# The first narrowing operation of the attention stage: on ScalarE and issued ahead, or on VectorE and in its turn

## The chip, the core and the metric

One core of a Trainium2 chip runs the whole program. The metric is device time in microseconds (us), lower is better. The core's engines are PE (matrix products; PEld is its weight load), DVE (VectorE), ACT (ScalarE), POOL (GpSimd) and SP (SyncE, which here issues the loads and stores). Each engine runs its own instructions strictly in the order in which the program lists them; an instruction whose input is late holds up everything behind it on that engine.

## The reference

```python
q_d = q.reshape(B, H, Sd, 4, D).mean(axis=3)            # k_d, v_d alike
out_up = np.repeat(sm_attn(q_d, k_d, v_d), 4, axis=2)   # attention on means of 4
mask = np.abs(pos[:, None] - pos[None, :]) < 4
out_local = softmax(where(mask, scale * q @ k.T, -1e9)) @ v
x = (out_up + out_local) as [2304, 512]                 # B=4, H=8, S=576, D=64
logits = x @ phi;  slots = softmax(logits, 0).T @ x     # 32 slots, 8 experts
slot_out[e] = relu(slots[e] @ w1[e]) @ w2[e]
y = softmax(logits, 1) @ slot_out
h = relu(y @ w_in);  result = (h * h) @ w_out           # w_in, w_out in float64
```

The last two weights come as 64-bit floats (512 x 2048 and 2048 x 512), and the kernel makes 32-bit floats of them.

## The kernel before

The work comes in four stages: attention (to about 200 us), the gate and the expert layers (to about 250 us), the first part of the last feed-forward layer, and its main loop, which is half of the span and almost all PE.

**Attention** is 16 units u, each one pair of heads of one batch. A unit passes through a software pipeline of about four steps; step s (lines 701 to 723) works on units s to s-4 at once. `ORDER` lists what one step issues, a letter each: V, D, A are the value products, their scaling on ACT (`xd`, line 530) and the sum on DVE (`xt`, line 538); T transposes q and k on PE (`tr`) and copies them out on ACT (`qk`, line 384); P pairs the heads of the next unit (`qp` on ACT, `kp` on DVE, line 373); Q and L and 4 are loads of q and k, of v in windows (`vw`), and of v in groups of 4 (`v`, used on POOL in line 484, whose sum `vd` DVE finishes in line 490). The last three letters are l (loads of weights that later stages need, `LOADN` of them), and c, which calls `narrow_next` (line 277) as often as `CONV[s]` says. All loads go through SP's queue in program order. SP waits at a load until its buffer is free; the load of q, for one, waits until ACT has made `qp` of the unit whose buffer it takes.

**Narrowing** a weight piece (128 x 512 doubles) takes five operations (`narrow`, line 206): the absolute value of the high words (line 213, ACT), a clamp (line 214), a shift with a mask (line 215), the sign (line 216) and the low bits (line 217), the last four on DVE. Pieces are narrowed two at a time, a *turn*: `NORDER` gives the turns, of which the first four, eight pieces of w_in, lie in attention. `narrow_turn` issues one operation of both pieces at each call. `narrow_ahead` takes the next turn, if its loads have been issued, and issues its first operation at once; it is called when a turn begins, and again right after the second operation of the current turn (line 268). So a turn's first operation is issued two to four calls ahead of its second.

```python
yield nc.scalar.activation(out=dst, in_=hi.bitcast(F32), func=AF.Abs)
...
if count[0] == 2:
    narrow_ahead()
```

`xq` is None until a pool of that name is opened in the expert stage (line 894); it stays None through all of attention, and is set for the later turns.

Of the kernel before, what the change touches and what calls it, by code (L numbers as in the profile page):

```python
# [9 lines left out]
F32 = mybir.dt.float32  # L10
# [3 lines left out]
AF = mybir.ActivationFunctionType  # L14
ALU = mybir.AluOpType
# [20 lines left out]
MAG_HI = 1.875 * 2.0 ** 16 - 2.0 ** -7  # L36
FILL = {0: 8, 1: 16, 2: 10, 3: 0, 16: 5, 17: 2, 18: 2}
FILLN = 0
CONV = {3: 1, 4: 1, 5: 1, 6: 1, 7: 1, 8: 1, 9: 1, 10: 0, 11: 2, 12: 1, 13: 2, 14: 1, 15: 2}
FILLT = {16: 4, 17: 6, 18: 8}  # L40
TCH = 384
LOOK = 2
# [29 lines left out]
def attention_moe_ffn_kernel(  # L72
# [12 lines left out]
    nc = tc.nc  # L85
# [120 lines left out]
    def narrow(dst, raw):  # L206

        hi, lo = raw[:, :, 1], raw[:, :, 0]  # L210
        di = dst.bitcast(I32)
        two, sel2 = nc.vector.tensor_scalar, nc.vector.scalar_tensor_tensor
        yield nc.scalar.activation(out=dst, in_=hi.bitcast(F32), func=AF.Abs)
        yield two(out=dst, in0=dst, scalar1=MAG_LO, scalar2=MAG_HI, op0=ALU.max, op1=ALU.min)
        yield two(out=di, in0=di, scalar1=3, scalar2=0x3FFFFFF8, op0=ALU.logical_shift_left, op1=ALU.bitwise_and)
        yield sel2(out=di, in0=hi, scalar=-0x40000000, in1=di, op0=ALU.bitwise_and, op1=ALU.bitwise_or)
        yield sel2(out=di, in0=lo, scalar=29, in1=di, op0=ALU.logical_shift_right, op1=ALU.bitwise_or)

    def narrow_win(i, j):
        if (j, i // 2) not in win:  # L220
            pool, tag = place = min((x for x in free if x[0] is (wa if j < 2 else ring)), key=lambda x: x[0] is wa and x[1])
            free.remove(place)
            win[j, i // 2] = pool.tile([128, 2, FF // 4], F32, tag=tag, name=f"win{j}_{i // 2}")
        yield from narrow(win[j, i // 2][:, i % 2], got["win", i, j])
        done("win", i, j)
# [3 lines left out]
    def narrow_wout(f):  # L229
        w32[f] = xq.tile([128, DM], F32, tag="w32", bufs=W32, name=f"w32_{f}")  # L230
        yield from narrow(w32[f], got["wout", f, 0])
# [7 lines left out]
    current, count, ahead = [], [0], []  # L239

    def ready(y):
        if y[0] == "o":
            return ("wout", int(y[1:]), 0) in got and xq is not None
        return ("win", int(y[1]), int(y[3])) in got

    def narrow_ahead():

        if ahead or not turns or not all(ready(y) for y in turns[0]):
            return
        if len(w32) + sum(y[0] == "o" for y in turns[0]) > W32:  # L250
            return
        for y in turns.popleft():
            ahead.append((y, narrow_wout(int(y[1:])) if y[0] == "o" else narrow_win(int(y[1]), int(y[3]))))
        for y, z in ahead:
            next(z)

    def narrow_turn():
        if not current:
            narrow_ahead()
            if not ahead:  # L260
                return False
            current.extend(ahead)
            ahead.clear()
            count[0] = 1
        count[0] += 1
        for y, z in current:
            next(z)
        if count[0] == 2:
            narrow_ahead()
        if count[0] == 5:  # L270
            for y, z in current:
                next(z, None)
            current.clear()
            count[0] = 0
        return True

    def narrow_next(n=1):
        for _ in range(n):
            narrow_turn()

    def narrow_to(x):

        wanted = lambda y: y == f"o{x}" if isinstance(x, int) else y[0] == "w" and int(y[3]) <= int(x[1:])
        while any(wanted(y) for y, z in current + ahead) or any(wanted(y) for t in turns for y in t):
            assert narrow_turn()
# [4 lines left out]
    with tc.tile_pool(name="att", bufs=1, side="right") as ap:  # L290
# [410 lines left out]
        for s in range(3, NU):  # L701
# [6 lines left out]
            for x in ORDER:  # L708
# [9 lines left out]
                if x == "c":  # L718
                    narrow_next(CONV.get(s, 0))
                if x == "P" and s == NU - 2:  # L720
# [147 lines left out]
    for e in range(NE):  # L868
# [23 lines left out]
        if e == LBE:  # L892
            lb_scope.close()
            xq = ctx.enter_context(tc.tile_pool(name="slots", bufs=1, side="right", reuse_waits="tile"))
# [196 lines left out]
```

## Time and profile before

| | us |
|---|---|
| median of 3 runs (lowest, highest) | 486.12 (484.34, 487.14) |
| the profiled execution's own time | 488.41 |
| its span, first to last instruction | 486.6 |
| PE, DVE, ACT, POOL busy | 431.8, 312.9, 261.8, 96.7 |

Busy shares are means over stages that differ: after 280 us PE is hardly ever idle, before 200 us every engine waits at times. So the part to read is the stretch in which the changed instructions stand, about 35 to 200 us. The profiled execution's span is 1.8 us shorter than its time, and its time is 2.3 us above the median.

### The profile page before, as it was taken

The numbers are of one execution on the slowest core, as the hardware profiler recorded it, in microseconds if no ns is written. First come the engines' busy times: TensorE is split into PE (matmuls) and PEld (weight loads), VectorE is DVE, ScalarE is ACT, GpSimd is POOL, SyncE is SP. The second block draws the span as 40 slices with busy tenths as digits, with TensorE's granted clock in tenths as the row PEclk, the third lists the DMA queues.
The fourth block names the chain that finished last, engine by engine and source line by source line (L and its number), as shares of the span: only waits on it lengthen the run. The fifth ranks groups of instructions, "written<-read, shape, count | busy, mean of one in ns | idle before, by whom it ended". The sixth has DMA issues, their size and how long they took to land.

```text
span 486.6 us, 10625 instructions
## 1 busy us (share of the span) xinstructions
PE 431.8 (89%) x4098; PEld 330.7 (68%) x4098; DVE 312.9 (64%) x675; ACT 261.8 (54%) x657; POOL 96.7 (20%) x128
## 2 busy tenths in 40 slices
PE   4799788496996794999987999999999999999996
PEld 3577565384675663644455787878888888888885
DVE  5669778495997983313259899875555545546452
ACT  3576564564765542212466988786545444444442
POOL 4336555363544643002000000000000000000000
PEclk9687889797897896789999999999999999999999
DMA  7898988688897879799999200000200100100001
GB/s 146 204 277 210 202 235 203 178 217 206 191 234 194 249 208 286 252 362 399 393 408 409 112 0 3 0 1 24 107 1 1 66 0 8 58 1 30 35 2 65
DMA packets 65780, 75.13 MB, mean 154 GB/s; under 512 B 23873, under 2 KB 47169, under 8 KB 65729
## 3 DMA queue, kind: packets, MB, share of 16 engines
q1 hardware_dynamic: 65584, 74.31, 51.7%
q8 instruction: 32, 0.52, 0.5%
q14 instruction: 20, 0.16, 0.1%
q10 hardware_dynamic: 144, 0.13, 0.1%
HBM read 69.71 MB, written 4.72 MB: 153 GB/s over the span
## 4 chain that ended last, share of the span: by engine, by line
PE 62%; DVE 15%; DMA 9%; issue 6%; POOL 3%; ACT 2%; SPq 2%; DVEq 0%; POOLq 0%; ACTq 0%
PE po L1020 37%; DMA q<-in_q_dram 4%; PE hp L828 4%; PE so L852 3%; PE up L960 3%; DMA v<-in_v_dram 3%; DVE vd L490 2%; POOL v L484 2%; DMA k<-in_k_dram 2%; DVE kz L401 2%; PE tr L383 2%; PE av L512 1%; PE av L525 1%; PE sd L435 1%; PE ptp L478 1%
## 5 line engine op out<-in xcount | busy, mean ns | idle before, releaser
L1020 PE MATMUL po<-wparts,ghi 128*128 128x512 f32 x576 | 150.6, 395 | 4.3 <-DVE wparts L918 4.2
L1020 PEld LDWEIGHTS po<-wparts,ghi 128*128 128x128 f32 x576 | 107.2, 189 | 26.8 <-DVE wparts L918 6.6
L965 ACT ACTIVATE r<-up 128x384 f32<-128x384 f32 x96 | 47.0, 489 | 72.0 <-PE up L960 67.1
L1020 PE MATMUL po<-wparts,glo 128*128 128x512 f32 x288 | 82.2, 393 | 0.5 <-DVE glo L973 0.5
L969 DVE TENSOR_TENSOR r<-r 128x384 f32<-128x384 f32 x64 | 35.7, 558 | 58.4 <-ACT ghi L968 58.4
L973 DVE TENSOR_TENSOR glo<-r,ghi 128x384 fp32r<-128x384 f32 x94 | 52.4, 558 | 16.5 <-ACT ghi L972 10.4
L1020 PEld LDWEIGHTS po<-wparts,glo 128*128 128x128 f32 x288 | 54.4, 189 | 12.5 <-DVE glo L973 1.2
L968 ACT ACTIVATE ghi<-r 128x384 fp32r<-128x384 f32 x66 | 34.7, 526 | 2.1
L960 PE MATMUL up<-cst,ast 128*128 128x384 f32 x96 | 33.0, 346 | 0.4 <-DVE ast L951 0.4
L484 POOL TENSOR_TENSOR v<-v 72x512 f32<-72x512 f32 x16 | 20.7, 1293 | 51.7 <-DMA v<-in_v_dram 39.6
L490 DVE TENSOR_TENSOR vd<-v 72x256 f32<-72x256 f32 x16 | 16.0, 999 | 20.8 <-POOL v L484 20.8
L463 POOL TENSOR_TENSOR pl<-el,sm 64x350 f32<-64x350 f32 x30 | 24.4, 813 | 18.8 <-DVE sm L455 12.1
L525 PE MATMUL av<-pdt,vd 72*64 72x144 f32 x128 | 13.9, 348 | 15.8 <-DVE vd L490 15.8
L383 PE MATMUL tr<-ident,qp 96*128 96x96 f32 x96 | 20.1, 299 | 7.2 <-ACT qp L373 6.9
L384 ACT COPY qk<-tr 128x384 f32<-128x384 f32 x48 | 22.1, 523 | 6.6 <-PE tr L383 5.5
L512 PE MATMUL av<-pt,vw 64*64 64x58 f32 x640 | 23.8, 230 | 0.2 <-DVE xt L538 0.2
L512 PEld LDWEIGHTS av<-pt,vw 64*64 64x64 f32 x640 | 21.6, 144 | 3.2 <-issue 1.5
L478 PE MATMUL ptp<-ident,pl 128*128 128x128 f32 x80 | 15.6, 338 | 7.7 <-ACT qk L384 6.3
L383 PE MATMUL tr<-ident,kp 96*128 96x96 f32 x96 | 19.5, 293 | 2.3 <-DVE kp L373 2.3
L960 PEld LDWEIGHTS up<-cst,ast 128*128 128x128 f32 x96 | 18.1, 189 | 4.6 <-DVE ast L951 0.7
L401 DVE COPY kz<-qk 64x586 f32<-64x586 f32 x32 | 20.4, 636 | 1.0 <-ACT qk L384 0.8
L525 PEld LDWEIGHTS av<-pdt,vd 72*64 72x64 f32 x128 | 8.8, 160 | 17.8 <-DVE vd L490 12.3
(186 smaller groups left out, 726.9 us busy)
## 6 DMA issues: line engine op xcount, KB each, us to landing
w<-in_moe_w_dram SPq DMA_DIRECT2D x64, 512.0 KB
win<-in_moe_w_in_dram SPq DMA_DIRECT2D x16, 512.0 KB
wout<-in_moe_w_out_dram SPq DMA_DIRECT2D x16, 512.0 KB
q<-in_q_dram SPq DMA_DIRECT2D x16, 288.0 KB
k<-in_k_dram SPq DMA_DIRECT2D x16, 288.0 KB
v<-in_v_dram SPq DMA_DIRECT2D x16, 288.0 KB
out_dram<-o SPq DMA_DIRECT2D x17, 256.0 KB
vw<-in_v_dram SPq DMA_DIRECT2D x32, 128.0 KB
```

The lines of the kernel that those rows point to most:

```text
L383: nc.tensor.transpose(t[:, j, r], st[nm][:, i, r].rearrange("p h d -> p (h d)"), ident[0:96, 0:96])
L401: (nc.scalar.copy if h < KZACT else nc.vector.tensor_copy)(out=kz[r, h], in_=k2[r])
L484: nc.gpsimd.tensor_tensor(out=v4[:, :, 0], in0=v4[:, :, 0], in1=v4[:, :, 1], op=ALU.add)
L490: nc.vector.tensor_tensor(out=vd.rearrange("p h a d -> p (h a) d"), in0=v4[:, :, 0, 0], in1=v4[:, :, 0, 1], op=ALU.add)
L512: nc.tensor.matmul(av[a][rr, 2 * HQ * i:2 * HQ * i + 2 * HQ].rearrange("p (f c) -> p f c", f=2), vw[rr, 2 * i + a], ptv[rr, i, :, a, 0:HQ] ...
L525: nc.tensor.matmul(dn[rr], st["vd"][:, h, a], st["pdt"][:, a, :, h], start=(a == 0), stop=(a == 1), skip_group_check=True,)
L960: nc.tensor.matmul(t, ast[:, 128 * f:128 * f + 128], cst[:, c * n:c * n + n], start=True, stop=True)
L965: nc.scalar.activation(out=r, in_=t, func=AF.Relu)
L968: nc.scalar.activation(out=ghi, in_=r, func=AF.Square)
L969: nc.vector.tensor_tensor(out=g, in0=r, in1=r, op=ALU.mult)
L973: nc.vector.tensor_tensor(out=glo, in0=g, in1=ghi, op=ALU.subtract)
L1020: nc.tensor.matmul(po[c][i], a[:, 128 * i:128 * i + 128], w[f], start=(f == 0 and w is whi and a is ghi), stop=(f == NF - 1 and a is glo), ...
```

## The change

Where `xq` is None, that is in attention, the first operation of `narrow` is a bitwise AND on DVE (clearing the sign bit of the high word) in place of the ACT absolute value; `narrow_turn` ends its call after issuing it when it begins a new turn; and `narrow_ahead` is not called after the second operation. A turn so takes five calls where it took four. Four turns now need 20 calls where they needed 16: `CONV` has three more, one each in steps 8, 12 and 15, and of the three calls after step 15 two had found nothing to do before and one does now. So the same eight pieces are still done within attention. Later turns are as before.

```diff
-CONV = {3: 1, 4: 1, 5: 1, 6: 1, 7: 1, 8: 1, 9: 1, 10: 0, 11: 2, 12: 1, 13: 2, 14: 1, 15: 2}
+CONV = {3: 1, 4: 1, 5: 1, 6: 1, 7: 1, 8: 2, 9: 1, 10: 0, 11: 2, 12: 2, 13: 2, 14: 1, 15: 3}
...
-        yield nc.scalar.activation(out=dst, in_=hi.bitcast(F32), func=AF.Abs)
+        if xq is None:
+            yield two(out=di, in0=hi, scalar1=0x7FFFFFFF, scalar2=None, op0=ALU.bitwise_and)
+        else:
+            yield nc.scalar.activation(out=dst, in_=hi.bitcast(F32), func=AF.Abs)
...
     def narrow_turn():
         if not current:
+            new = not ahead
             narrow_ahead()
...
             count[0] = 1
+            if new and xq is None:
+                return True
         count[0] += 1
         for y, z in current:
             next(z)
-        if count[0] == 2:
+        if count[0] == 2 and xq is not None:
             narrow_ahead()
```

The order of instructions moves on ACT and DVE only; PE, POOL and SP keep theirs. Lines behind 213 stand 3 to 6 lines further down in the changed kernel.

ACT at the end of step 7, before: the last copies of that step, the first operation of the third turn (both pieces), then step 8's `xd`, the copies out of the transposes, and `qp`.

```order
L566 COPY xk_1270<-xp_1280 128x4x128
L569 COPY xr_1271<-xrp_1286 64x128
L213 ACTIVATE win_0_1300<-win_1_935 128x512
L213 ACTIVATE win_0_1300<-win_1_1294 128x512
L530 ACTIVATE xd<-av_0_1303 128x288
L384 COPY qk_136<-tr_0_1330 128x2x2x96
L384 COPY qk_136<-tr_1_1336 128x2x2x96
L384 COPY qk_136<-tr_2_1342 128x2x2x96
L373 COPY qp_1351<-q_1172 96x6x64 x2
```

The same place now:

```order
L572 COPY xk_1265<-xp_1275 128x4x128
L575 COPY xr_1266<-xrp_1281 64x128
L536 ACTIVATE xd<-av_0_1295 128x288
L390 COPY qk_136<-tr_0_1322 128x2x2x96
L390 COPY qk_136<-tr_1_1328 128x2x2x96
L390 COPY qk_136<-tr_2_1334 128x2x2x96
L379 COPY qp_1343<-q_1167 96x6x64 x2
```

Both ACTIVATE of line 213 are gone from between step 7 and step 8; nothing stands in their place on ACT.

DVE at the end of step 8, before: the normalisation, the second operation's follower of the second turn (line 215, both pieces), then step 9's `xt` and `kp`.

```order
L454 TENSOR_SCALAR sm_1390<-sm_1390 128x3
L455 RECIPROCAL sm_1390<-sm_1390 128x3
L215 TENSOR_SCALAR win_1_602<-win_1_602 128x512 x2
L538 TENSOR_TENSOR xt_1516<-av_0_1471,xd 128x5x58
L538 TENSOR_TENSOR xt_1516<-av_1_1472,xd 128x5x58
L373 COPY kp_1522<-k_1359 96x6x64 x2
```

The same place now:

```order
L460 TENSOR_SCALAR sm_1382<-sm_1382 128x3
L461 RECIPROCAL sm_1382<-sm_1382 128x3
L214 TENSOR_SCALAR win_1_1461<-win_0_329 128x512
L214 TENSOR_SCALAR win_1_1461<-win_0_327 128x512
L217 TENSOR_SCALAR win_1_1461<-win_1_1461 128x512 x2
L544 TENSOR_TENSOR xt_1511<-av_0_1466,xd 128x5x58
L544 TENSOR_TENSOR xt_1511<-av_1_1467,xd 128x5x58
L379 COPY kp_1517<-k_1351 96x6x64 x2
```

The new first operation (line 214 of the changed kernel) and the clamp (its line 217) of the second turn stand here now, two pairs where one stood. Step 12 has the same shape for the third turn.

DVE at the end of attention, before: the last operation of the fourth turn, then the `xt` of unit 14 and the `vd` of unit 15.

```order
L217 SCALAR_TENSOR_TENSOR win_1_2002<-win_1_1465,win_1_2002 128x512
L217 SCALAR_TENSOR_TENSOR win_1_2002<-win_1_1633,win_1_2002 128x512
L538 TENSOR_TENSOR xt_2864<-av_0_2820,xd 128x5x58
L538 TENSOR_TENSOR xt_2864<-av_1_2821,xd 128x5x58
L490 TENSOR_TENSOR vd_2877<-v_2812 72x256
```

The same place now:

```order
L219 SCALAR_TENSOR_TENSOR win_1_2683<-win_1_1457,win_1_2683 128x512
L219 SCALAR_TENSOR_TENSOR win_1_2683<-win_1_1628,win_1_2683 128x512
L544 TENSOR_TENSOR xt_2862<-av_0_2818,xd 128x5x58
L544 TENSOR_TENSOR xt_2862<-av_1_2819,xd 128x5x58
L220 SCALAR_TENSOR_TENSOR win_1_2683<-win_1_1457,win_1_2683 128x512
L220 SCALAR_TENSOR_TENSOR win_1_2683<-win_1_1628,win_1_2683 128x512
L496 TENSOR_TENSOR vd_2877<-v_2810 72x256
```

The fourth turn ends one call later: its last pair stands between the last `xt` shown and `vd`, where nothing stood.

## Rows read from the trace of the kernel before

**Rows 1.** The page, busy time by engine, and the chain by engine.

```profile
PE 431.8 (89%) x4098; PEld 330.7 (68%) x4098; DVE 312.9 (64%) x675; ACT 261.8 (54%) x657; POOL 96.7 (20%) x128
...
PE 62%; DVE 15%; DMA 9%; issue 6%; POOL 3%; ACT 2%; SPq 2%; DVEq 0%; POOLq 0%; ACTq 0%
```

**Rows 2.** Stretches: length, busy time by engine, granted clock, DMA share, GB/s.

```profile
20.00:80.00 60.00, 51.74 (x806) 39.89 (x799) 47.56 (x109) 38.42 (x122) 29.78 (x31) 0.83 0.91 231
100.00:180.00 80.00, 67.89 (x1086) 51.16 (x1076) 67.12 (x144) 45.29 (x145) 41.66 (x43) 0.87 0.87 222
85.00:90.00 5.00, 0.01 (x1) 0.00 (x0) 0.91 (x1) 0.18 (x1) 1.83 (x2) 0.83 0.78 253
90.00:95.00 5.00, 3.69 (x22) 2.96 (x23) 2.98 (x8) 3.81 (x10) 1.79 (x3) 0.50 0.27 83
95.00:100.00 5.00, 5.00 (x106) 4.08 (x108) 4.85 (x12) 3.94 (x14) 2.67 (x4) 0.99 0.74 146
210.00:240.00 30.00, 29.78 (x449) 15.14 (x442) 9.14 (x36) 9.01 (x35) 3.44 (x12) 0.98 1.03 383
```

**Rows 3.** Line 213: durations (min/median/max) and what it waited for.

```profile
L213 ACT ACTIVATE win<-win x16: 656/672/689, 35.7 to 292.2; 128x512 f32<-128x512 f32 x16
...
DMA win<-in_moe_w_in_dram: 8.6, 1
```

**Rows 4.** Timeline of ACT: start, length, instruction, idle before and releaser.

```profile
80.52 0.68 ACT L213 ACTIVATE win<-win 128x512 f32<-128x512 f32 x1
89.82 0.66 ACT L213 ACTIVATE win<-win 128x512 f32<-128x512 f32 x1 [8.62 <-DMA win<-in_moe_w_in_dram]
...
110.35 0.93 ACT L373 COPY qp<-q 96x384 f32<-96x384 f32 x2 [2.67 <-DMA q<-in_q_dram]
```

**Rows 5.** Timeline of PE around the same time.

```profile
84.19 0.82 PE L413 MATMUL s<-kz,qk 128*29 128x70 f32 x40 [0.95 <-DVE kz L401]
91.31 1.30 PE L478 MATMUL ptp<-ident,pl 128*128 128x128 f32 x5 [6.31 <-ACT qk L384]
92.54 1.71 PE L435 MATMUL sd<-qkd 64*64 64x144 f32 x12
...
101.11 0.95 PE L435 MATMUL sd<-qkd 64*64 64x144 f32 x12
```

**Rows 6.** Timeline of SP's queue around the same time.

```profile
85.31 0.40 SPq L154 DMA_DIRECT2D win<-in_moe_w_in_dram  x1
85.76 0.42 SPq L160 DMA_DIRECT2D w<-in_moe_w_dram  x1
92.78 0.34 SPq L336 DMA_DIRECT2D q<-in_q_dram  x1
```

**Rows 7.** SP's waits, 60 to 200 us: total, times, longest.

```profile
SPq L336 <- ACT qp L373: 6.5, 1, 6.5
```

**Rows 8.** The chain of waits, 84 to 135 us: start, length, what.

```profile
101.39 8.88 DMA q<-in_q_dram
```

**Rows 9.** Narrowing on DVE, 35 to 190 us: busy us, mean ns, idle before.

```profile
L216 DVE SCALAR_TENSOR_TENSOR win<-win,win 128x512 int32<-128x512 int32 x8 | 8.3, 1077 | 0.0
...
L215 DVE TENSOR_SCALAR win<-win 128x512 int32<-128x512 int32 x8 | 6.4, 838 | 0.0
L214 DVE TENSOR_SCALAR win<-win 128x512 f32<-128x512 f32 x8 | 5.1, 678 | 0.0
```

**Rows 10.** The same tile on DVE, whole span: ns min/median/max.

```profile
L214 DVE TENSOR_SCALAR win<-win x16: 396/420/1136, 40.1 to 298.7; 128x512 f32<-128x512 f32 x16
```

**Rows 11.** Timeline of DVE: pairs of narrowing operations, and waits of `vd`.

```profile
84.46 1.45 DVE L214 TENSOR_SCALAR win<-win 128x512 f32<-128x512 f32 x2
...
117.55 1.35 DVE L490 TENSOR_TENSOR vd<-v 72x256 f32<-72x256 f32 x1 [3.88 <-POOL v L484]
132.31 1.98 DVE L217 SCALAR_TENSOR_TENSOR win<-win,win 128x512 int32<-128x512 int32 x2
150.66 1.35 DVE L490 TENSOR_TENSOR vd<-v 72x256 f32<-72x256 f32 x1 [3.08 <-POOL v L484]
...
193.04 0.42 DVE L490 TENSOR_TENSOR vd<-v 72x256 f32<-72x256 f32 x1 [5.80 <-POOL v L484]
```

## The prediction

> **What bounds the kernel now.** I read the page first. PE is busy 89% of the span, and the chain that ended last runs through PE for 62% of it [rows 1]. That is no answer for this change, since the changed instructions stand in attention alone. So the next view is busy time by stretch [rows 2]: the reader is to see that in attention no engine is full. From 100 to 180 us PE is busy 67.9 of 80 us, VectorE 67.1, ScalarE 45.3, and the DMA engines carry a share of 0.87; from 20 to 80 us the share is 0.91. Weighted by length that is (0.91 x 60 + 0.87 x 80) / 140 = 0.887. Attention is paced mostly by its loads, with VectorE close behind. From 210 to 240 us PE is busy 29.8 of 30 us: the expert stage is bound by PE, so whatever attention gives or takes reaches the end unchanged.
>
> The same view shows one odd place: from 85 to 90 us PE is busy 0.01 of 5 us, and from 90 to 95 us the DMA share falls to 0.27. The rows of line 213 say why. Its operation takes 0.672 us and waited once, 8.6 us, for a load of w_in [rows 3]. The ScalarE timeline shows the wait: the first piece of the third turn runs at 80.52, the second only at 89.82 [rows 4]. Its load was not issued until 85.31 [rows 6]; the operation stood in ScalarE's queue ahead of a load that SP had not reached yet. Behind it in that queue stand `xd`, the copies out of the transposes and `qp`. PE, which had started its score products at 84.19, then sat idle 6.31 us for those copies [rows 5], and SP held the next load of q for 6.5 us until `qp` was made [rows 7], from about 86.2 to 92.78 [rows 6]. That is where the DMA engines ran dry.
>
> **The change, part by part.**
>
> *Eight operations leave ScalarE*: 8 x 0.672 = 5.4 us [rows 3]. ScalarE is busy 45.3 of 80 us, so the work by itself I cost at nothing: its idle time hides it, and if that cover were gone the credit would be at most those 5.4 us.
>
> *The wait goes.* The new first operation of the third turn stands on VectorE in step 12, some 50 us after its load was issued, and I find no first operation left that stands within a step of its load, so no wait moves to VectorE. What is late next is the load of q and the loads behind it. Two bounds for the gain. Above: PE's gap of 6.31 us, and then the work behind it that ran at a granted clock of 0.50 (1.2 GHz, after an idle stretch) from 90 to 95 us [rows 2, 5]: a group of products took 1.71 us there and 0.95 us one unit later [rows 5]. With the two groups beside it at the same ratio some 1.7 us, so 8.0 us in all. Below: what the DMA engines can win back. Against 0.887 the three stretches from 85 to 100 us lack 0.107, 0.617 and 0.147 [rows 2], times 5 us: 0.5 + 3.1 + 0.7 = 4.4 us. I take 4.4 us, because the next long piece of the chain is again a load, 8.88 us for q from 101.39 [rows 8]: there the pace is set by bytes, not by PE.
>
> *Eight operations come to VectorE.* The trace has no AND that reads every second word. The nearest rows: a clamp or shift of the same size in the same places costs 0.678 and 0.838 us on average [rows 9], with 0.396 us as the least [rows 10], and the operation that also reads every second word, but two inputs, 1.077 us [rows 9]. So 8 operations cost between 3.2 and 8.6 us; I take the mean of the two one-input rows, 0.76 us, 6.1 us in all, since they are the same kind of instruction. The spread within one line, 0.396 to 1.136 us, comes from GpSimd's work beside it. The Trainium skill (VectorE: DVE Perf Modes, What auto-detection actually checks) has a one-source operation between places in SBUF take two elements a cycle when the outermost dimension is even, and asks for no step of one at this width; by that rule the AND costs what the clamp costs, 6.1 us for the eight, and without it 8.6 us. No row of this trace has a one-source operation that reads with a step of two, so this stays an estimate.
>
> How much of the 6.1 us is on the path? The pairs of steps 8, 12 and 15 stand ahead of waits that VectorE has anyway: its `vd` waits 3.88 us at 117.55, 3.08 us at 150.66 and 5.80 us at 193.04, each for GpSimd's sum, which waits for the load of v [rows 11]. A pair costs about 1.45 us (84.46) [rows 11], less than any of them, so these are covered as long as the loads keep the pace; without that cover they cost their 6.1 us. The pair of step 3 takes the place of a clamp. The rest is a shift by one call: in steps 7, 11 and 14 a pair of line 217 (1.98 us at 132.31 [rows 11]) stands where a clamp pair stood (1.45 us), 0.53 us more, and in steps 5, 9 and 13 it is the other way round. The step 7 one falls into the vanished wait; for steps 11 and 14 I see no wait right behind, and count 2 x 0.53 = 1.1 us.
>
> *The last turn ends one call later*, with 2 us of work between `xt` and the `vd` at 193.04, under its wait of 5.80 us [rows 11]: nothing. Without that wait it would be 2 us. No load changes its place in SP's queue.
>
> **The sum.** Minus 4.4 plus 1.1 is minus 3.3 us. Against the profiled execution (span 486.6, time 488.41) that makes 485.1; that execution stands 2.3 us above the median of 486.12, and against the median it is **482.8 us**.
>
> **The rivals.**
>
> *A, the gain is mostly hidden by loads.* If q's load is issued 6.5 us earlier but queues behind the pieces of w_in and w2 issued at 85.31 and 85.76 [rows 6], it lands little earlier, and the 8.88 us of the next load [rows 8] grow by what was saved. For: the share is 0.78 even during the wait. Against: it is 0.27 right after, and that is time nothing used. Then only part of the 3.1 us of that stretch is won, say two thirds, 2.1 us, less 1.1: about 485.1, no change that can be told.
>
> *B, VectorE becomes the pace: slower.* In the last third of the stretch VectorE is busy 4.85 of 5 us [rows 2], and over 100 to 180 us 84%. If all the added work lands on the path at the dearer price, 8.6 us, the 4.4 us gained are more than spent: plus 4.2, 490.3 us. It decides from the point where more than 6.8 us (4.4 + 2.4) of added VectorE time is uncovered, which needs the waits of `vd` [rows 11] to shrink to nothing. Against: they are waits for loads, and the loads stay. The Trainium skill (Perfetto Trace Analysis, Optimizing Scalar/DVE Operations) speaks for this rival: with VectorE saturated it advises giving work to ScalarE, and this change does the reverse. Busy 84% against ScalarE's 57%, the trace agrees with half of it: VectorE is the busier engine, but not full.
>
> *C, the wait only moves.* If a new first operation still meets a load in flight, VectorE would stall as ScalarE did, and the time would stay near 486 us plus the 1.1. The distance between loads and operations in the order speaks against it.
>
> **How the numbers follow.** The forecast's own range runs from the full 8.0 us gained less 1.1 (479.2) to where it can no longer be told from no change (483.7). A measurement of this kernel can tell about 0.5%, 2.4 us, from no change. I give the forecast 0.62, A and C together 0.27, B 0.11. The range takes the forecast's whole own range and A up to a little beyond no change: 479.2 to 486.8. It leaves out B and a little of the others. Chances: faster 0.62, same 0.27, slower 0.11.
>
> **What would show it.** Right: in the new profile line 213 has no wait for a load, PE has no gap of 6 us near 85 us, the DMA share in 90 to 95 us is near 0.9, SP's wait for `qp` of 6.5 us is gone, and the first expert product starts about 3 us earlier. The AND takes 0.4 to 1.1 us. Wrong for A: the gap is gone but the waits for q and v between 95 and 125 us are longer by as much. Wrong for B: `vd` no longer waits for GpSimd, and PE waits more for VectorE in every unit behind step 8. If attention ends at the same time although both the gap is gone and `vd` still waits, my DMA bound was wrong.

## The result and the profile after

| | before | changed |
|---|---|---|
| median of 20 runs, us | 485.40 (481.08 to 489.06) | 482.82 (475.13 to 487.25) |
| mean of the 20, us | 485.21 | 481.91 |
| the profiled execution: time, span | 488.41, 486.6 | 483.15, 481.4 |
| first product behind attention (`stp`) starts, us | 203.86 | 198.25 |

The ratio of the changed kernel to the one before is 0.9869, with an interval of 0.9832 to 0.9906: faster, by 6.4 us at 485.4, which makes 479.0 us. That ratio leaves out the runs that stand over 1.5% above the fastest of their kernel, and the changed kernel has single runs down to 475.13 us, so it gives a larger gain than all the runs do, whose medians are 2.6 us and whose means 3.3 us apart. Two later comparisons of the same pair gave 0.9972 (0.9929 to 1.0016) and 0.9897 (0.9839 to 0.9956). In what follows a "difference" is that of the means of all runs to the kernel before in the same comparison, with its standard error. For the changed kernel the three are -3.3 ± 0.9, -1.5 ± 1.0 and -4.8 ± 1.3 us; weighted by their errors -2.9 ± 0.6.

Behind `stp` the two executions take 282.7 and 283.2 us, so what was won was won in attention. The page of the changed kernel, busy time and chain, beside [rows 1]:

```profile
PE 432.6 (90%) x4098; PEld 330.6 (69%) x4098; DVE 318.6 (66%) x683; ACT 257.6 (54%) x649; POOL 97.0 (20%) x128
...
PE 53%; DVE 21%; issue 13%; POOL 6%; ACT 4%; DMA 3%; POOLq 0%; SPq 0%; DVEq 0%; ACTq 0%
```

VectorE has 5.7 us more work and ScalarE 4.2 us less. In the chain the share of loads went from 9% to 3% and that of VectorE from 15% to 21%; in one more execution of the kernel before and two more of the changed one (runs before_again, after_again, after_third) loads take 8%, 6% and 7% and VectorE 18%, 17% and 21%, so much of that shift belongs to the single executions. The same stretches as in [rows 2] (length, busy PE, PEld, DVE, ACT, POOL, granted clock, DMA share, GB/s):

```profile
20.00:80.00 60.00, 47.96 (x743) 36.54 (x747) 47.72 (x108) 35.90 (x118) 28.70 (x30) 0.89 0.92 225
100.00:180.00 80.00, 68.34 (x1065) 51.55 (x1063) 67.19 (x144) 42.20 (x138) 41.80 (x43) 0.85 0.87 219
85.00:90.00 5.00, 3.98 (x83) 3.07 (x80) 4.84 (x11) 2.12 (x6) 1.18 (x1) 1.00 0.74 179
90.00:95.00 5.00, 3.36 (x55) 2.74 (x56) 3.25 (x7) 2.78 (x12) 3.87 (x4) 0.87 1.05 265
95.00:100.00 5.00, 5.00 (x62) 4.02 (x62) 4.89 (x12) 3.09 (x7) 1.82 (x3) 0.50 0.72 149
210.00:240.00 30.00, 29.68 (x436) 14.79 (x435) 7.62 (x30) 9.17 (x34) 3.33 (x12) 1.00 1.04 398
```

The hole from 85 to 95 us is filled: PE is busy 3.98 of 5 us where it was busy 0.01, and the DMA share from 90 to 95 us is 1.05 where it was 0.27. The other stretches read much as before. The timelines of ScalarE, PE and SP's queue at that place, beside [rows 4 to 6]:

```profile
85.00 0.93 ACT L379 COPY qp<-q 96x384 f32<-96x384 f32 x2
```

```profile
84.88 0.82 PE L419 MATMUL s<-kz,qk 128*29 128x70 f32 x40 [0.53 <-DVE kz L407]
85.63 0.77 PE L484 MATMUL ptp<-ident,pl 128*128 128x128 f32 x5
```

```profile
86.51 0.40 SPq L154 DMA_DIRECT2D win<-in_moe_w_in_dram  x1
86.96 1.15 SPq L160 DMA_DIRECT2D w<-in_moe_w_dram  x1
88.21 0.41 SPq L342 DMA_DIRECT2D q<-in_q_dram  x1
```

`qp` now runs before the load of w_in is even issued; `ptp` follows the score products at once, where it stood 6.31 us behind; the load of q follows w2's by 0.1 us, where it stood some 6.5 us behind. What the new operations cost (narrowing on VectorE by form, 35 to 200 us: busy us, mean ns, idle before; then the spread of the AND), beside [rows 9, 10]:

```profile
L219 DVE SCALAR_TENSOR_TENSOR win<-win,win 128x512 int32<-128x512 int32 x8 | 7.8, 1014 | 0.0
...
L214 DVE TENSOR_SCALAR win<-win 128x512 int32<-128x512 int32 x8 | 5.8, 766 | 0.0
L217 DVE TENSOR_SCALAR win<-win 128x512 f32<-128x512 f32 x8 | 5.4, 709 | 0.0
L218 DVE TENSOR_SCALAR win<-win 128x512 int32<-128x512 int32 x8 | 5.1, 677 | 0.0
```

```profile
L214 DVE TENSOR_SCALAR win<-win x8: 397/766/1137, 39.3 to 175.3; 128x512 int32<-128x512 int32 x8
```

The AND takes 0.766 us on average and 0.397 us at the least, close to the clamp's 0.709 us here and its least of 0.396 us before [rows 10]. And what VectorE's `vd` waits for GpSimd (35 to 200 us: total, times, longest), first before, then changed:

```profile
DVE vd L490 <- POOL v L484: 20.8, 7, 5.8
```

```profile
DVE vd L496 <- POOL v L490: 15.9, 8, 2.9
```

The waits that were to cover the added work are 4.9 us shorter in this pair, and still there. Other executions give 23.2 us for the kernel before and 20.1 and 17.9 us for the changed one, so the 4.9 us are not the added work alone.

### The profile page after: what moved, and what is told of

Same layout as the page of the kernel before. It is cut to its first block, busy times and chain, and to the rows that moved or that the text cites. A ratio compares the mean times of both kernels' runs of the same rounds, so it can differ in the third digit from the quotient of the medians.

```text
span 481.4 us, 10625 instructions
## 1 busy us (share of the span) xinstructions
PE 432.6 (90%) x4098; PEld 330.6 (69%) x4098; DVE 318.6 (66%) x683; ACT 257.6 (54%) x649; POOL 97.0 (20%) x128
## 4 chain that ended last, share of the span: by engine, by line
PE 53%; DVE 21%; issue 13%; POOL 6%; ACT 4%; DMA 3%; POOLq 0%; SPq 0%; DVEq 0%; ACTq 0%
PE po L1026 38%; PE hp L834 4%; DVE vd L496 4%; PE up L966 3%; PE so L858 3%; POOL v L490 3%; DVE kz L407 3%; POOL pd L477 2%; DMA k<-in_k_dram 2%; DVE sm L460 1%; DVE win L220 1%; DVE sm L461 1%; DVE sm L466 1%; DVE win L219 1%; PE av L531 1%
## 5 line engine op out<-in xcount | busy, mean ns | idle before, releaser
L971 ACT ACTIVATE r<-up 128x384 f32<-128x384 f32 x96 | 47.0, 490 | 72.0 <-PE up L966 67.2
L1026 PEld LDWEIGHTS po<-wparts,glo 128*128 128x128 f32 x288 | 54.2, 189 | 12.4 <-DVE glo L979 1.1
L496 DVE TENSOR_TENSOR vd<-v 72x256 f32<-72x256 f32 x16 | 17.8, 1114 | 15.9 <-POOL v L490 15.9
L389 PE MATMUL tr<-ident,kp 96*128 96x96 f32 x96 | 20.1, 301 | 2.5 <-DVE kp L379 2.5
L433 ACT ACTIVATE el<-el 128x350 f32<-128x350 f32 x16 | 8.0, 497 | 25.7 <-DVE el L428 25.7
L379 ACT COPY qp<-q 96x384 f32<-96x384 f32 x32 | 14.8, 513 | 11.5 <-DMA q<-in_q_dram 11.4
```

Source lines behind the costliest of these rows:

```text
L389: nc.tensor.transpose(t[:, j, r], st[nm][:, i, r].rearrange("p h d -> p (h d)"), ident[0:96, 0:96])
L496: nc.vector.tensor_tensor(out=vd.rearrange("p h a d -> p (h a) d"), in0=v4[:, :, 0, 0], in1=v4[:, :, 0, 1], op=ALU.add)
L971: nc.scalar.activation(out=r, in_=t, func=AF.Relu)
L1026: nc.tensor.matmul(po[c][i], a[:, 128 * i:128 * i + 128], w[f], start=(f == 0 and w is whi and a is ghi), stop=(f == NF - 1 and a is glo), ...
```

## Experiments

Three things were open: whether the vanished wait is the whole difference; why a wait on one engine costs what it costs; and whether VectorE's added work costs anything. A letter in an expectation names a theory that is stated there. The difference and the ratio are to the kernel before:

| kernel | median us | difference, us | ratio (interval) |
|---|---|---|---|
| act_in_turn | 483.94 | -2.7 ± 0.7 | 0.9984 (0.9952 to 1.0016) |
| ahead_later | 483.56 | -3.0 ± 1.1 | 0.9960 (0.9920 to 0.9999) |
| dve_ahead | 484.14 | -3.3 ± 0.9 | 0.9998 (0.9952 to 1.0044) |
| and_twice | 483.00 | -4.1 ± 0.8 | 0.9947 (0.9914 to 0.9980) |
| q_free | 484.42 | -1.4 ± 0.8 | 0.9997 (0.9961 to 1.0033) |
| act_stall | 483.93 | -2.5 ± 0.9 | 0.9948 (0.9907 to 0.9989) |
| act_stall_again | 486.74 | -0.7 ± 0.9 | 0.9972 (0.9930 to 1.0013) |
| act_mid | 487.59 | +1.5 ± 1.0 | 1.0008 (0.9969 to 1.0047) |
| act_long | 494.18 | +7.1 ± 1.5 | 1.0132 (1.0055 to 1.0209) |
| act_long_q | 492.76 | +5.9 ± 1.2 | 1.0151 (1.0098 to 1.0203) |
| dve_stall | 490.69 | +4.0 ± 0.9 | 1.0113 (1.0060 to 1.0166) |
| wait_back | 485.92 | -0.5 ± 0.9 | 0.9998 (0.9961 to 1.0036) |
| before_again | 487.06 | +0.9 ± 1.0 | 1.0031 (0.9995 to 1.0067) |
| after_again | 484.23 | -1.5 ± 1.0 | 0.9972 (0.9929 to 1.0016) |
| after_third | 482.34 | -4.8 ± 1.3 | 0.9897 (0.9839 to 0.9956) |

**One part of the change at a time.** act_in_turn keeps the operation on ScalarE, but in its turn. From the changed kernel:

```diff
-        if xq is None:
-            yield two(out=di, in0=hi, scalar1=0x7FFFFFFF, scalar2=None, op0=ALU.bitwise_and)
-        else:
-            yield nc.scalar.activation(out=dst, in_=hi.bitcast(F32), func=AF.Abs)
+        yield nc.scalar.activation(out=dst, in_=hi.bitcast(F32), func=AF.Abs)
```

> The changed kernel, but the first operation stays on ScalarE (the absolute value), in its turn. Theory T (the gain is the vanished wait of ScalarE for a load that was issued after the operation): as fast as the changed kernel or up to 1.1 us faster, so 4 to 8 us below before; no idle time of ScalarE before line 213's operation until a load of w_in. Rival V (the gain is ScalarE's 5.4 us less work, the engine change itself): like before, within 1.5 us.

ahead_later stays with the kernel before and its ScalarE, and only issues ahead one call later:

```diff
-        if count[0] == 2:
+        if count[0] == (3 if xq is None else 2):
             narrow_ahead()
```

> The kernel before, with the next turn's first operation issued ahead after the third operation of a turn instead of the second, within attention; it stays on ScalarE, VectorE's and SP's order are untouched. Theory T: 4 to 8 us faster than before, since the third turn's operation now stands one step behind its load; PE's gap near 85 us gone. If the gain comes from the drain of attention (the last turn's place, the buffers) and not from the wait: within 1.5 us of before.

dve_ahead is the other half: the AND on VectorE as in the change, but issued ahead as before.

> The kernel before, with the first operation as an AND on VectorE, still issued ahead. Theory T: the wait moves to VectorE, where it holds up vd, xt and kp as well: not faster than before, 0 to 6 us slower; VectorE idle some 5 us or more until the load of w_in near 85 us. Rival V: 4 to 6 us faster than before.

The differences are -2.7, -3.0 and -3.3 us, like the changed kernel's own, though theory T had asked for 4 to 8 us of gain in the first two and for none in dve_ahead. By the ratio, which goes by fewer runs, act_in_turn and dve_ahead cannot be told from the kernel before, and ahead_later just can. In the first two no wait for a load of w_in is left, so by the means it is enough to take the operation out of that one place, and ScalarE's lighter work (rival V) is not needed. In dve_ahead VectorE inherits the wait. Its timelines of VectorE, PE and SP's queue:

```profile
88.64 1.25 DVE L214 TENSOR_SCALAR win<-win 128x512 int32<-128x512 int32 x1 [4.59 <-DMA win<-in_moe_w_in_dram]
```

```profile
90.69 0.73 PE L559 MATMUL lgt<-xt,phis 128*32 128x128 f32 x16 [5.61 <-DVE xt L541]
```

```profile
84.94 0.41 SPq L339 DMA_DIRECT2D q<-in_q_dram  x1
91.19 0.32 SPq L339 DMA_DIRECT2D k<-in_k_dram  x1
```

PE still loses 5.61 us, VectorE waits 4.59 us, and SP still holds a load, now that of k; yet by the means the time is as good. In this run a gap of PE of that length cost nothing that could be told.

**VectorE's work doubled.** and_twice issues each AND twice:

```diff
         if xq is None:
+            two(out=di, in0=hi, scalar1=0x7FFFFFFF, scalar2=None, op0=ALU.bitwise_and)
             yield two(out=di, in0=hi, scalar1=0x7FFFFFFF, scalar2=None, op0=ALU.bitwise_and)
```

> The changed kernel with every AND in attention issued twice on VectorE (the same result). Eight more operations of 0.77 us, 6 us of VectorE. Theory T with covered VectorE work: 0 to 2 us slower than the changed kernel. Rival B (VectorE sets the pace): 5 to 9 us slower than the changed kernel, so no longer faster than before.

Its narrowing on VectorE and its waits of `vd`:

```profile
L215 DVE TENSOR_SCALAR win<-win 128x512 int32<-128x512 int32 x8 | 5.8, 721 | 0.3
...
L214 DVE TENSOR_SCALAR win<-win 128x512 int32<-128x512 int32 x8 | 4.3, 544 | 0.0
```

```profile
DVE vd L497 <- POOL v L491: 12.9, 6, 3.0
```

Ten us of AND instead of 5.8, and the time is no longer: 1.2 us under the changed kernel's -2.9, within the errors. The waits of `vd` are 12.9 us here; act_in_turn and ahead_later, with no AND on VectorE, have 19.7 and 17.9 us, and the changed kernel 15.9 to 20.1 us in three executions. So the waits are longer than the added work in all of them, but how much of it they took up these spreads do not show. The time says that it is covered.

**The loads freed from the stall.** q_free is the kernel before, but unit 10's q and k, whose loads stood behind ScalarE's stall, get two buffers of their own, which the loads of weights lack until then; the order on every engine stays:

```diff
-    free = deque((ring, f"r{i}") for i in range(NRING))
+    free = deque((ring, f"r{i}") for i in range(NRING - 2))
...
-                place = dict(q="q", k="k") if u != 1 else dict(q=f"r{NRING - 2}", k=f"r{NRING - 1}")
+                place = dict(q="q", k="k") if u not in (1, 10) else dict(q=f"r{NRING - 2}", k=f"r{NRING - 1}")
...
+                if x == "P" and s == 9:
+                    free.extend((ring, f"r{NRING - y}") for y in (2, 1))
```

> The kernel before, order of every engine unchanged, but the q and k of unit 10 (the loads that stood behind ScalarE's stalled queue) get two buffers of their own, so that SP need not wait for qp there. ScalarE still waits about 8.6 us for the w_in load and PE still has its gap of about 6 us. Theory S (the price was SP's held queue, so the DMA engines ran dry): no 6.5 us wait of SP on qp, DMA share from 90 to 95 us above 0.7, and 2.5 to 4.5 us faster than before, although both compute engines stall as they did. Theory T (the price was the idle time of ScalarE and PE itself): within 1.5 us of before.

ScalarE, PE, SP's queue and the DMA share (last but one column of the stretch) in q_free:

```profile
90.09 0.66 ACT L213 ACTIVATE win<-win 128x512 f32<-128x512 f32 x1 [10.28 <-DMA win<-in_moe_w_in_dram]
```

```profile
91.58 1.30 PE L478 MATMUL ptp<-ident,pl 128*128 128x128 f32 x5 [8.67 <-ACT qk L384]
```

```profile
85.08 0.46 SPq L336 DMA_DIRECT2D q<-in_q_dram  x1
```

```profile
90.00:95.00 5.00, 3.42 (x20) 2.69 (x21) 2.74 (x7) 4.00 (x10) 1.47 (x2) 0.50 1.05 178
```

The stall is there, the held load is not, and the DMA engines do not run dry. The difference is -1.4 ± 0.8: it lies between the two theories, and the changed kernel on the same chip gave -1.5 ± 1.0 (after_again). What it says of the price of a stall comes below.

**A stall of a chosen length.** act_stall puts 13 scratch operations on ScalarE where the old operation stood, into the changed kernel; act_mid has 18 and act_long 26 of them:

```diff
+    scr = cp.tile([128, 512], F32, name="scr")
+    nc.gpsimd.memset(scr, 0.0)
...
+                if x == "c" and s == 7:
+                    for _ in range(13):
+                        nc.scalar.activation(out=scr, in_=scr, func=AF.Abs)
```

> The changed kernel with 13 extra scratch operations on ScalarE (about 8.7 us by 0.67 us each) at the end of step 7, where the old operation stood; the result is unchanged. Both theories give back what the change won: SP is held again for qp by about 6 us, PE has a gap of 5 us or more, attention ends 3 to 5 us later than in the changed kernel, and the time is 2.5 to 4.5 us above it, at the time of before. If instead the time stays within 1.5 us of the changed kernel, the vanished wait was not what the change won, and the gain comes from elsewhere (the end of attention, or the work taken from ScalarE).

> The kernel with 13 extra operations on ScalarE (8.6 us) once more, beside the others on one chip. Theory W with a drain (a stall of fixed length ends before the queued loads have landed, so that the DMA engines lose less): 0 to 1.5 us above the changed kernel, and SP's wait for qp 5 to 6 us. If the first reading was chance, it stands 2 to 4 us above, as the kernel with the wait put back does.

> 18 extra operations on ScalarE (11.9 us), between the 13 that cost nothing to tell (8.6 us) and the 26 that cost 8 to 10 us (17.2 us); the result is unchanged. Theory E (some 7 to 9 us are covered, then each us costs one): 3 to 5 us above the changed kernel, SP's wait for qp 8 to 10 us. If the cover is nearer 12 us: within 1 us of the changed kernel.

> The changed kernel with 26 extra scratch operations on ScalarE (17.2 us by 0.66 us each) at the end of step 7; the result is unchanged. 13 of them (8.6 us) cost nothing that could be told. Theory E (loads have a lead of some 6 to 9 us over the engines, and a stall costs only what goes beyond it): SP waits 14 to 15 us for qp, attention ends 7 to 10 us later than in the changed kernel, and the time is 7 to 10 us above it. Theory N (a stall in one queue is always made up by the next units): within 3 us of the changed kernel.

How long the scratch work stands on ScalarE (timeline; the second run of the 13, then the 18 and the 26):

```profile
82.94 8.57 ACT L730 ACTIVATE scr<-scr 128x512 f32<-128x512 f32 x13
```

```profile
79.94 11.88 ACT L730 ACTIVATE scr<-scr 128x512 f32<-128x512 f32 x18
```

```profile
83.25 17.17 ACT L730 ACTIVATE scr<-scr 128x512 f32<-128x512 f32 x26
```

The first run of the 13 seemed to cost nothing (-2.5), against its expectation; the second stood at -0.7. Together, weighted by their errors, they are -1.5 ± 0.6. Against the changed kernel's -2.9 the three lengths cost 1.4 ± 0.9, 4.4 ± 1.2 and 10.0 ± 1.6 us. Taken from the lengths that leaves 7.2, 7.5 and 7.2 us: **at this place ScalarE can stand for some 7 us at no cost, and each us beyond costs about one.** Theory E held in that. The three agree better than their errors would have them. Against the changed kernel on the same chip (after_again, after_third) the two runs of the 13 cost -1.1 ± 1.1 and 4.1 ± 1.5 us and the 18 cost 6.3 ± 1.6 us, so what is covered can be anything from 4 to 10 us. The old stall lasted from the start of the first piece at 80.52 to the end of the second at 89.82 + 0.66 = 90.48 [rows 4], 9.96 us; less 7.3 that is 2.7 us, and the change won 2.9 ± 0.6.

**The same on VectorE.** dve_stall has 13 scratch operations (`scalar_tensor_tensor`) on VectorE at the same place instead.

> The changed kernel with 13 extra scratch operations on VectorE (about 9 to 14 us by 0.7 to 1.08 us each) at the end of step 7; the result is unchanged. Theory S: VectorE holds kp and so one load of k for some us, but not the load of q; as loads set the pace and vd has waits ahead of it, the time is at most 2 us above the changed kernel. Theory T, and the view that VectorE is the pace of attention: PE gets a gap of 5 us or more and the time rises by 4 us or more.

```profile
85.05 11.50 DVE L730 SCALAR_TENSOR_TENSOR scr<-scr 128x512 f32<-128x512 f32 x13
```

They take 11.50 us and cost 6.9 ± 1.1 against the changed kernel (4.0 + 2.9). The other theory (T) was right on this one: 11.50 - 6.9 leaves 4.6 us of cover, or 6.0 us against the changed kernel on the same chip (-1.5). That VectorE's cover is less than ScalarE's 7 is therefore not shown. dve_ahead fits the longer cover: there VectorE stood from its first AND at 83.63 to the end of the second at 89.89, 6.3 us, at no cost.

**A long stall with the loads freed.** act_long_q is act_long with the two buffers of q_free.

> The same 26 extra operations on ScalarE, but the q and k of unit 10 get buffers of their own, so that SP does not wait for qp behind the stall. Theory S (a stall costs what it holds back of the loads): at least 5 us faster than with the loads held, at most 4 us above the changed kernel, though PE stands idle as long, 12 us or more. Theory T (the idle time of the compute engines is the cost): within 2 us of the kernel with the loads held.

The stretch of 20 us in which the stall stands and the next, in act_long and then in act_long_q (DMA share last but one):

```profile
80.00:100.00 20.00, 6.61 (x128) 4.71 (x124) 5.45 (x11) 16.60 (x28) 4.71 (x5) 0.76 0.47 118
100.00:120.00 20.00, 18.58 (x310) 14.75 (x310) 17.61 (x40) 13.98 (x43) 10.11 (x11) 0.88 0.71 172
```

```profile
80.00:100.00 20.00, 8.02 (x124) 5.40 (x123) 5.41 (x11) 15.82 (x27) 4.71 (x6) 0.67 0.71 151
100.00:120.00 20.00, 17.69 (x290) 14.15 (x290) 16.80 (x38) 15.03 (x45) 10.02 (x11) 0.79 0.60 146
```

The two differ by 1.2 ± 1.6 us, not by the 5 that theory S (the price of a stall is what it holds back of the loads) had asked for. But the two buffers did not free the loads for long. SP's next load of v waited 11.4 us for `vd`, and the DMA engines ran dry all the same, a little later:

```profile
SPq L367 <- DVE vd L498: 12.6, 2, 11.4
```

```profile
95.00:100.00 5.00, 0.00 (x0) 0.00 (x0) 0.00 (x0) 4.75 (x9) 0.00 (x0) 0.50 0.05 12
```

So S missed its number, and its idea was not tested here: what is let go early (share 0.71 instead of 0.47) is missing later (0.60 instead of 0.71).

**Two ways to price a stall.** One is the rule above, the length less 7.3 us. The other is the prediction's, the work that the DMA engines lack, here over 80 to 120 us. The stretch in the kernel before, the changed kernel, q_free and dve_ahead:

```profile
80.00:120.00 40.00, 28.11 (x483) 22.36 (x481) 28.49 (x61) 19.99 (x61) 18.85 (x21) 0.86 0.80 199
```

```profile
80.00:120.00 40.00, 32.66 (x512) 25.93 (x512) 31.57 (x64) 19.78 (x60) 20.69 (x23) 0.80 0.89 211
```

```profile
80.00:120.00 40.00, 29.12 (x507) 22.84 (x505) 29.66 (x69) 22.56 (x71) 19.84 (x21) 0.87 0.87 202
```

```profile
80.00:120.00 40.00, 31.14 (x501) 24.70 (x498) 33.14 (x71) 21.97 (x69) 19.60 (x21) 0.81 0.81 200
```

The changed kernel's share is 0.89, 0.89 and 0.91 in its three executions. Against 0.90 the kernel before lacks 0.10 x 40 = 4.0 us, act_mid (0.75) 6.0, act_long (0.59) 12.4 and act_long_q (0.65) 10.0; they cost 2.9, 4.4, 10.0 and 8.8 us, so the loads' way follows the costs too, 1 to 2.5 us too high. The two ways part in q_free and dve_ahead. In q_free ScalarE stood from 79.14 to 90.75, 11.6 us, which by the stall's rule costs 4.3 us, and the loads lack 1.2 us; it cost 1.5 ± 1.0 (0.1 ± 1.0 against after_again). In dve_ahead the loads lack 3.6 us, and it cost nothing (-0.4 ± 1.1). So each way fails in one run, and wait_back, below, is priced higher by both: 4.9 us by the stall (12.2 us) and 6.8 us by the loads (0.73), for 2.4 ± 1.0 (4.3 ± 1.5 against after_third). Which of the two sets the price stays open.

**The wait alone, put back.** wait_back adds to the changed kernel one scratch operation, at the old place, that reads the w_in piece whose load was issued last:

```diff
+                if x == "c" and s == 7:
+                    late = [y for y in got if y[0] == "win"][-1]
+                    nc.scalar.activation(out=scr, in_=got[late][:, :, 1].bitcast(F32), func=AF.Abs)
```

> The changed kernel with one extra scratch operation of 0.67 us on ScalarE at the end of step 7 that reads the w_in piece whose load was issued last: the vanished wait alone is put back, at its old place, and nothing else; the result is unchanged. Theory W (that wait is the whole difference): ScalarE waits 8 to 10 us for that load, SP holds the load of q 5 to 7 us for qp, DMA share from 90 to 95 us under 0.4, and the time is 2 to 4 us above the changed kernel, that is within 1 us of before. Theory R (the difference comes from the other edits, the work off ScalarE or the new places on VectorE): within 1 us of the changed kernel although the wait is there.

> The changed kernel a third time, as the base of the three others on this chip: 1.5 to 3.5 us below before in the mean. Attention ends at 199 to 204 us.

ScalarE, PE, SP's queue and the stretch from 90 to 95 us in wait_back:

```profile
90.87 0.66 ACT L730 ACTIVATE scr<-win 128x512 f32<-128x512 f32 x1 [11.50 <-DMA win<-in_moe_w_in_dram]
```

```profile
92.37 1.30 PE L486 MATMUL ptp<-ident,pl 128*128 128x128 f32 x5 [8.35 <-ACT qk L392]
```

```profile
SPq L344 <- ACT qp L381: 7.4, 1, 7.4
```

```profile
90.00:95.00 5.00, 2.63 (x17) 2.16 (x17) 2.31 (x6) 4.00 (x10) 1.15 (x1) 0.50 0.17 60
```

Every sign of the old stall is back with this one instruction, and so is the time: -0.5 ± 0.9 to before, +4.3 ± 1.5 to the changed kernel on the same chip (means 485.80 and 481.53), and +2.4 ± 1.0 to the -2.9 of all three comparisons. Theory W held; theory R, which gave the gain to the other edits, fell. ScalarE's idle time of 11.50 us holds more than the old 8.62: in this execution it begins 1.8 us earlier, 0.7 us of that because no first piece runs ahead of it, and ends 1.05 us later.

**The comparison itself.** before_again and after_again are the two kernels unchanged.

> The kernel before once more, unchanged, for a second profile and as a test of the comparison itself: ratio 1 within 0.003. ScalarE's wait for the w_in load (8 to 9 us) and SP's wait on qp (5 to 7 us) are there again. If the late load of v of the last unit (14.9 us behind the one ahead of it, 10.7 in the changed kernel) belongs to the kernel, it is there again (over 14); if it was chance, it is 10 to 12.5 us, and this profile's attention ends at 201 to 204 us instead of 205.97.

> The changed kernel once more, on the same chip as the three others, for a common base and a second profile. Both theories: 2.5 to 4.5 us below before, no wait of ScalarE for w_in in attention, attention ends at about 200.4 us. If the late load of v of the last unit (191.75 us before, 186.78 us after) was chance, its place varies by some us between profiles of the same kernel; if it belongs to the change, it is near 186.5 us here too.

Equal kernels read +0.9 ± 1.0 apart. after_again missed its 2.5 to 4.5 us with -1.5 ± 1.0, and its profiled execution takes 488.55 us, as long as the 488.41 us of the kernel before, though the wait is gone: one execution does not show a gain of this size. One thing makes up part of that. GpSimd's work on the last unit's v starts 14.9 and 13.8 us behind that of the unit ahead in the two executions of before, and 10.7, 11.2 and 13.4 us in three of the changed kernel. So it is later by 2.7 us in one execution than in another of the same kernel; whether the change has a part in it, and which of the loads queued beside it makes it late, stays open.

No variant beats the changed kernel by more than its error, so none is offered in its place.

## Why the prediction was right, and where it was wrong

- **The direction and its cause** were right. By the means of all runs the wait of line 213 is, within the errors, the whole difference: the four variants without it on ScalarE gain 2.7 to 4.1 us, and with it alone put back the gain is gone.
- **The size, "I take 4.4 us"**, is the step that failed. The first comparison's ratio is worth 6.4 us and a time of 479.0 us, below the forecast's 479.2 to 483.7. As the 1.1 us for VectorE turned out to be nothing, the term measured 6.4 us there, between my bounds of 4.4 and 8.0, of which I took the lower; all runs of three comparisons give 2.9 ± 0.6. Why the ratio gives twice as much as all the runs stays open; single runs of the changed kernel go down to 475 and 477 us in two of the comparisons, and none of the kernel before's below 479.
- **How the term was worked out** (the work that the DMA engines lack) follows the cost of most stalls within 2.5 us, and the length of the stall less 7.3 us does as well (9.96 - 7.3 = 2.7 us). dve_ahead speaks against the first and q_free against the second. So I had no ground to let the loads alone set the price, and what does set it stays open.
- **That the median came out at 482.82**, as forecast, is luck: the 3.3 us were taken from a median of 3 runs, 486.12, and the 20 runs of the kernel before have 485.40.
- **"Plus 1.1 us" for VectorE** was wrong: with twice the ANDs the time is 1.2 ± 1.0 us less, so no cost shows, also none for the pairs of steps 11 and 14.
- **The AND at 0.76 us** measured 0.766. The mean is made of two sizes, four ANDs of 0.40 us and four of 1.13 to 1.14 us; in the trace each of the long ones has at least 0.85 us of GpSimd's work beside it and each of the short ones 0.14 us, as the prediction had it of the spread. Its 6.1 us for the eight is the mean of the clamp and the shift; the clamp's own row [rows 9] gives 5.4 us. The Trainium skill (VectorE: DVE Perf Modes, What auto-detection actually checks) names no step of one among the conditions of the mode that takes two results a cycle from a single source; the trace agrees, with a least time of 397 ns beside the clamp's 396 [rows 10].
- **The cover by the `vd` waits** held in so far as they never vanished (12.9 us with sixteen ANDs). That they shrink by the added work is not shown, as they spread by 4 us between executions of one kernel.
- **"Then the work behind it at a granted clock of 0.50"**, part of the upper bound, does not show as a gain: the changed kernel's profile has a stretch at 0.50 too, five us later, with PE busy 5.00 of 5 us, and over 80 to 120 us the granted clock is 0.80, 0.87 and 0.86 in three executions of it, 0.86 and 0.84 in two of the kernel before.
- **Rival A** (the loads hide the gain) did not fall altogether. The hole is used, with a DMA share of 1.05 from 90 to 95 us. But the sign that it named is there: over 30 to 200 us ScalarE waits 8.7, 9.8 and 8.4 us for q in three executions, where it was 4.4 and 4.2 us; between 95 and 125 us GpSimd waits 12.9, 12.9 and 5.6 us for v, where it was 2.7 and 7.3 us. Its gain of 2.1 us, without the 1.1, cannot be told from 2.9 ± 0.6.
- **Rival C** (the wait only moves) fell as no wait for a load of w_in is left. **Rival B** (VectorE becomes the pace) fell with and_twice. The Trainium skill (Perfetto Trace Analysis, Optimizing Scalar/DVE Operations) advises the reverse of this change where VectorE is saturated. It was not saturated here, with 67.2 of 80 us busy from 100 to 180 us. Still, dve_stall lost 6.9 us by 11.5 us of work in one piece, where some 10 us of ANDs spread over attention cost nothing.

## What to carry to other kernels

In a program of in-order queues, look not only at how long an instruction takes but at whether its input can still be under way when its turn comes: one operation of 0.67 us, issued ahead for safety, held a whole engine for 9 us. Here a stall did not cost its length; find out by scratch work of two or three lengths how much of it the surrounding stage absorbs, and count only the rest. Look also at what the stall does to the loads: the two could not be told apart here. And where the runs of a kernel spread by 2%, repeat the comparison before believing the size of a gain of 1%.

## What the runs showed of the hardware that was not expected

An operation on VectorE that reads every second 32-bit word (the AND) costs about what ones that read all of them cost: in the changed kernel 0.397 us at the least, beside 0.412 for the clamp and 0.394 for the shift. PE's granted clock fell to 0.50 (1.2 GHz) behind the gap of 8.35 us in wait_back, and it was 1.00 from 85 to 100 us in one execution of the changed kernel in which PE was busy 4.05, 3.21 and 4.48 us of each 5:

```profile
90.00:95.00 5.00, 3.21 (x60) 2.67 (x60) 4.83 (x9) 3.59 (x13) 3.63 (x4) 1.00 1.00 249
```

And executions of one and the same kernel differ by up to 12 us (475.13 to 487.25); in the profiled ones of the changed kernel the stage behind attention takes 283.2, 283.3 and 283.2 us, while attention ends at 198.25, 203.46 and 199.84 us. In these three the spread is all attention's; the two of before take 282.7 and 280.4 us behind it.
